# Attention and a mixture of experts on one core: another list of steps, in which no operation changes

## Chip, cores and metric

The kernel runs on one core of a Trainium2 chip. The metric is device time in microseconds from the start to the end of one execution; smaller is better. The engines are TensorE (PE in the rows, with its weight loads as PEld), VectorE (DVE), ScalarE (ACT), GpSimd (POOL) and SyncE (SP), which issues the transfers here.

## What is computed

Causal attention over 8 batches of 8 heads, 576 positions and 64 elements, with a bias from running sums of s; its output, laid out as (8, 576, 512), is the input of a layer of four experts, each a causal attention of its own with 64 elements, of which each position uses the two that a gate ranks highest.

```python
scores = scale * np.matmul(q, k.transpose(0, 1, 3, 2))
cum = np.cumsum(np.maximum(s, 0.0), axis=-1)
bias = -(cum[:, :, :, None] - cum[:, :, None, :])
scores = np.where(causal, -1000000000.0, scores + np.minimum(bias, 0.0))
scores = scores - np.max(scores, axis=-1, keepdims=True)
attn = np.exp(scores)
attn = attn / (np.sum(attn, axis=-1, keepdims=True) + 1e-09)
attn_out = np.matmul(attn, v)
...
logits = x @ w_gate
topk = np.argpartition(-logits, K, axis=-1)[..., :K]
...
for e in range(E):
    q = x @ wq[e]
    k = x @ wk[e]
    v = x @ wv[e]
    ...
    ye = a @ v @ wo[e]
    out += mask[..., None] * w[:, :, kk:kk + 1] * ye
```

## The kernel before

The work is cut into 50 pairs of heads: four pairs for each of the 8 batches of the attention (phase 1), and, one batch later, two pairs of experts for each batch of the second layer (phase 2), whose q, k and v come from projections of the attention's output. Two empty pairs stand between where the last batch has no attention beside it. Slot n of the program, from -2 to 49, holds steps of several pairs, so that the engines always have more than one pair in work: the scores of pair n, the product with v of pair n-1, the maxima of pairs n+1 and n+2, and what comes before and after them.

For one pair the steps and their names in the list are these. Loads: `ld` (L571) brings q and k as "raw", L640 and L641 the q and k of the first pairs as "plain", `lv` (L581, L585) brings v. Splitting: every operand of a score is kept as a rounded high part, q1 and k1, and the rest, q2 and k2. `hi` makes the high parts (`h`, ACT, L679, L689, L720) and copies rows of running sums to k2 (L671); `lo` makes the rest (`l0` to `l3`, DVE, L736 for q and L750 for k in phase 1, L732 and L745 in phase 2) and copies parts with DMAs (L722 and others). Maxima: PE makes scores in bf16 (`m`, L769, and L787 for the diagonal pieces, tiles "mx"), DVE reduces them to a column (`M`, L799, tile "mcol"), PE transposes the nine columns (`mt`, L824), ACT copies them (`mA`, L828, tile "mr") and SP writes them as a row of q2 (`mq`, L841, or L835). Scores: seven banks per pair, each with two passes (`s`, L872 with the high parts and L877 with the rest, whose operands hold the row of maxima; L942 and L946 are the second and third kind of piece). Then ACT makes exponentials (`E`, L916, L918, L925), and POOL sets the upper triangle to zero (`b`, L955) and adds the tiles up into r (`d`, L969 to L977). PE multiplies with v (`v`, L1012, evicted by `V`, L1026) and, for two pairs at once, sums the rows (`a`, L1065, tile "sm", evicted by `A`, L1074). The sums go through DMAs (`r`, L1093, L1102, L1107) and a reciprocal (L1096) to a tile rb, and DVE multiplies with it (L1131). ACT and DVE split the product into a high part and the rest x (L1135 and L1144), and PE projects it (`p`, L1242; tiles "pq", "pw" and "po") to the experts' q and k, to v and the gate, and to the output. Twenty spare steps (`i`, L1486), each of three matmuls of 128x512 on a constant tile, stand in slot -2.

PSUM has eight banks: `take` gives the one that was free for longest, `give` puts one back when its eviction is written down. Which bank a matmul gets, and whose eviction it waits for, therefore follows from the list.

What sets the order of every engine and queue is one list, `ORDER` (lines 82 to 309): 3773 words "slot:step". The program walks through it and calls each step, and every engine and SP run their instructions in the order in which the steps issued them. The loop is:

```python
steps = {n: slot(n) for n in range(-2, N)}
for n, x in order(pairs):
    if x in steps[n]:
        steps[n].pop(x)()
```

Of the kernel before, what the change touches and what calls it, by code (L numbers as in the profile page):

```python
# [47 lines left out]
def pieces(kt, q0, q1):  # L48
# [45 lines left out]
    "2:s2 2:E2 2:b0 -2:i16 2:m4 1:V1 2:s1 2:E1 2:s4 1:m2 2:v0 2:m1 1:w0l 1:d0 2:m3 2:E4 2:d1 2:v3 2:a0 "
    "2:M4 3:lq 2:M3 2:M1 3:lk 1:M2 3:h2 2:a1 2:A1 3:w0l 2:lq 2:m0 3:hc 3:l3 2:A0 2:v1 3:lv 2:mt 2:mA 3:r0 "
    "2:b3 3:m3 3:h3 3:M3 2:v2 3:v0 2:v4 2:b1 2:v5 2:v6 2:v7 2:M0 3:r1 2:mq 2:b2 3:r2 2:d2 3:h1 3:h0 4:m4 "
    "2:m2 2:M2 3:r3 2:V0 3:m2 3:m1 2:V1 3:r4 3:s5 3:E5 3:l1 3:s6 3:E6 3:s0 3:E0 3:s3 3:E3 3:mt 3:mA 3:mq "
    "3:l0 3:l2 2:d0 3:s1 4:l0 4:h0 3:E1 3:s4 3:E4 3:s2 3:E2 3:v1 4:lv 3:v2 3:V0 4:m5 4:h2 3:v3 3:m0 4:M5 "
    "3:M0 2:d3 2:d4 4:lk 3:n0 4:w1f 3:N0 3:v4 4:m3 3:v5 3:M1 4:M4 4:s3 3:b0 4:M3 3:M2 3:n1 4:lq 4:l2 4:v0 "
    "4:E3 4:hc 4:ld 4:h1 3:b2 3:b4 3:b1 4:w0f 3:v6 3:v7 4:s0 4:E0 4:l1 3:o0 3:b3 4:s2 4:E2 4:s4 3:d0 4:mt "  # L100
    "4:E4 4:mA 4:s6 4:E6 3:V1 3:d1 4:h3 4:mq 4:l3 4:w1h 4:w1l 4:s1 3:d2 4:a0 3:d3 3:d4 4:a1 4:A0 4:A1 "
    "4:s5 5:m3 4:v3 4:v4 5:r0 4:E5 5:l2 5:hc 4:E1 4:m2 4:b3 5:r1 5:r2 5:r3 4:v1 4:v2 4:V0 5:lk 5:m5 5:M5 "
    "4:M2 4:v5 4:w0h 4:w0l 4:b1 5:r4 4:m1 5:v3 5:v4 5:m4 3:N1 4:b0 4:d1 5:h3 4:m0 4:v6 5:h0 4:b2 4:b4 "
    "5:s1 5:E1 4:M1 4:M0 5:M4 5:M3 5:h1 4:v7 5:v5 5:v6 5:v7 5:lq 5:s3 4:d2 4:V1 5:h2 4:d3 5:s5 5:E5 5:v0 "
    "5:v1 3:o1 5:v2 5:V0 5:V1 5:s6 5:E6 5:s4 5:E4 5:E3 5:n0 6:w0f 5:s2 4:d4 5:E2 5:s0 5:mt 5:mA 5:n1 5:N0 "
    "5:o0 5:N1 5:E0 5:b0 7:lv 6:lv 5:o1 5:O1 6:m3 6:m5 6:M3 6:M5 5:O0 6:w0h 5:m2 6:lq 5:m1 5:m0 5:M0 3:O1 "
    "5:b2 5:M1 6:m4 6:M4 5:M2 5:l1 5:d1 5:p2 5:P2 5:p0 5:l0 5:mq 5:p3 5:p1 3:O0 5:p6 5:P1 4:d0 6:mt 5:P0 "
    "6:lk 6:l2 6:w1f 5:lv 6:w1h 6:h0 6:l3 6:s6 5:d2 6:E6 6:s1 6:s3 6:E3 6:s2 5:P3 6:E2 6:mA 6:w0l 5:l3 "
    "6:h1 8:ld 5:b3 5:d3 6:mq 5:p4 6:E1 6:b3 6:s5 6:E5 6:b4 6:s0 6:E0 7:ld 6:s4 6:h3 7:lk 5:P6 5:p7 6:l0 "
    "7:l0 7:l1 5:p5 5:P5 5:P4 6:w1l 5:b1 5:d0 6:a0 6:A0 5:b4 5:d4 6:a1 6:A1 7:m3 7:m5 7:M5 5:P7 7:h1 6:l1 "  # L110
    "6:E4 7:r0 6:b2 7:hc 6:v3 6:h2 7:lq 6:v0 6:v1 6:v2 6:b0 6:v4 6:v5 6:v6 6:v7 6:V1 6:V0 6:d1 6:d2 6:m0 "
    "7:r1 7:r2 7:M3 9:ld 7:r3 7:r4 7:s6 7:E6 7:s5 7:E5 7:s0 6:d3 6:M1 6:M2 6:M0 8:h3 7:s3 7:E3 7:b2 6:d4 "
    "7:s1 7:E1 7:s2 7:E2 6:p1 6:P1 6:b1 7:b3 7:E0 7:s4 7:E4 7:b0 7:b1 7:d0 6:hc 7:M4 7:mt 7:mA 7:mq 6:p0 "
    "6:P0 7:h0 8:l1 8:m3 7:l3 7:m0 7:h2 8:m5 7:M0 8:h0 8:p0 7:M1 8:M3 8:M5 8:M4 7:p0 8:P0 8:J0 7:p1 7:d1 "
    "7:v3 7:v4 7:v5 7:l2 8:n0 8:h1 7:b4 8:h2 7:v6 7:v7 7:P1 7:P0 8:L0 8:g0 7:h3 7:M2 8:lq 7:v0 7:v1 7:v2 "
    "8:hc 7:V0 7:V1 7:d2 7:d3 7:d4 8:a1 6:d0 8:a0 8:A0 8:mt 8:mA 8:g2 8:A1 8:s3 8:n1 8:l2 8:lk 8:s0 8:s6 "
    "8:E3 8:E6 8:s5 8:E5 8:s4 8:E4 8:E0 8:l3 8:s1 9:h0 8:b0 8:s2 8:l0 8:N0 8:b1 9:h2 9:r0 9:r1 8:m0 8:mq "
# [12 lines left out]
    "12:m4 12:lq 12:M5 10:M2 11:M3 11:E5 11:m1 11:v6 11:b0 9:O0 11:m0 11:M1 11:v7 10:b1 10:d0 11:v0 13:ld "  # L130
    "11:v1 11:v2 12:m3 11:r1 11:m2 12:M4 11:V0 11:b1 11:d0 11:mt 9:O1 11:mA 12:M3 11:M2 11:b2 12:h2 10:d4 "
# [1458 lines left out]
```

## Time and profile before

| | |
|---|---|
| three runs | 638.54, 637.71, 638.65 us (median 638.54) |
| profiled execution | 637.61 us |
| its span, first to last instruction | 635.6 us |
| granted TensorE clock | 1.000 |
| PE, PEld, DVE, ACT, POOL busy | 99%, 78%, 80%, 74%, 63% |
| chain that ended last, by engine | PE 82%, DVE 7%, ACT 3%, DMA 3%, POOL 2%, SP 2%, issue 2% |

All times of rows come from the profiled execution and count from the first instruction. PE is the engine with the most work; its own rows are therefore read for gaps, and the other engines' rows for what stood behind a gap. The ends of matmuls in the trace are modelled, so an end may lie behind the start of the next one; the starts are the better mark.

### The profile page before, as it was taken

What the parts mean: (1) busy time and instruction counts of PE and PEld (TensorE: products, weight loads), DVE (VectorE), ACT (ScalarE), POOL (GpSimd) and SP (SyncE); (2) the same over time, 40 slices, a digit from 0 to 9 for tenths busy, and PEclk for the clock granted to TensorE, in tenths of its full rate; (3) what the DMA queues carried; (4) which work ended last, traced back from release to release, by engine and by line L of the source; (5) the groups of instructions that cost most, each with busy time, mean ns of one, the idle gap of its engine ahead of it and who ended that gap; (6) DMA issues with size and microseconds to landing.
All of it is one profiled execution on the core that took longest, in us unless ns stands there. A gap on an engine that the chain in (4) does not pass through costs nothing.

```text
span 635.6 us, 15994 instructions
## 1 busy us (share of the span) xinstructions
PE 626.7 (99%) x5517; PEld 498.5 (78%) x5521; DVE 510.9 (80%) x1493; ACT 473.1 (74%) x1159; POOL 401.8 (63%) x511
## 2 busy tenths in 40 slices
PE   8999999999999999999999999999999999999997
PEld 4566798778887888788887888878877878888875
DVE  6888878999978887895788978777878989865884
ACT  3698968857779668778678768887687877676665
POOL 9488568477846766587563886558655875845040
PEclk9999999999999999999999999999999999999999
DMA  8444454345545455574547445553535555333304
GB/s 213 126 136 125 145 153 124 101 119 136 157 127 151 132 133 147 134 188 109 147 119 188 126 124 152 169 145 110 140 89 165 162 134 129 91 98 83 88 1 166
DMA packets 53478, 83.91 MB, mean 132 GB/s; under 512 B 21700, under 2 KB 21700, under 8 KB 53398
## 3 DMA queue, kind: packets, MB, share of 16 engines
q1 hardware_dynamic: 53398, 82.90, 49.2%
q8 instruction: 44, 0.72, 0.5%
q14 instruction: 36, 0.29, 0.1%
HBM read 44.61 MB, written 10.16 MB: 86 GB/s over the span
## 4 chain that ended last, share of the span: by engine, by line
PE 82%; DVE 7%; ACT 3%; DMA 3%; POOL 2%; SPq 2%; issue 2%; DVEq 0%; ACTq 0%; POOLq 0%
PE pvp L1012 17%; PE pq L1242 14%; PE s L872 10%; PE s L877 9%; PE pw L1242 9%; PE po L1242 6%; PE mx L769 5%; PE sm L1065 4%; DVE sink L799 2%; PE mx L787 2%; DVE k L750 1%; PE po L1216 1%; DVE q L736 1%; DVE x L1144 1%; PE mt L824 1%
## 5 line engine op out<-in xcount | busy, mean ns | idle before, releaser
L799 DVE CUSTOM_DVE_ANT_0 sink<-mx,mask 128x64 bf16<-128x64 f32 (+7 forms) x432 | 168.7, 428 | 61.7 <-PE mx L787 28.0
L955 POOL TENSOR_SCALAR_AFFINE_SELECT p<-p 128x256 f32<-128x256 f32 (+1 forms) x192 | 93.8, 500 | 116.4 <-ACT p L916 94.2
L916 ACT ACTIVATE p<-s 128x512 f32<-128x512 f32 (+2 forms) x288 | 140.2, 521 | 24.8 <-PE s L946 11.6
L975 POOL TENSOR_TENSOR r<-r,p 128x640 f32<-128x640 f32 x92 | 125.4, 1364 | 5.3
L872 PE MATMUL s<-q,k 128*128 128x320 f32 (+3 forms) x460 | 125.5, 322 | 0.5 <-issue 0.3
L877 PE MATMUL s<-q,k 97*128 97x320 f32 (+3 forms) x460 | 122.3, 315 | 0.1
L1242 PE MATMUL pq<-x,wqkh 128*128 128x288 f32 x512 | 106.6, 300 | 1.3 <-DVE x L1144 1.1
L1012 PE MATMUL pvp<-p,v 128*64 128x320 f32 (+3 forms) x896 | 94.7, 344 | 0.0
L971 POOL TENSOR_TENSOR r<-p 128x640 f32<-128x640 f32 x46 | 74.6, 1623 | 24.1 <-ACT p L916 23.9
L872 PEld LDWEIGHTS s<-q,k 128*128 128x128 f32 x460 | 79.8, 189 | 10.9 <-issue 2.7
L1242 PEld LDWEIGHTS pq<-x,wqkh 128*128 128x128 f32 x512 | 82.0, 188 | 5.3 <-DVE x L1144 2.0
L877 PEld LDWEIGHTS s<-q,k 97*128 97x128 f32 x460 | 76.7, 190 | 1.3 <-DMA q<-mr 0.7
L1242 PE MATMUL pq<-x,wqkl 128*128 128x288 f32 x256 | 75.6, 295 | 0.0
L1012 PEld LDWEIGHTS pvp<-p,v 128*64 128x64 f32 x896 | 55.8, 137 | 23.5 <-issue 1.5
L955 POOL TENSOR_SCALAR_AFFINE_SELECT r<-p 128x256 f32<-128x256 f32 x48 | 25.8, 538 | 63.0 <-ACT p L918 62.7
L679 ACT ACTIVATE q<-raw 64x576 fp32r<-64x576 f32 x92 | 61.8, 678 | 2.3 <-PE s L905 1.1
L736 DVE TENSOR_TENSOR q<-raw,q 64x576 fp32r<-64x576 f32 x60 | 52.8, 893 | 6.0 <-ACT p L916 3.2
L750 DVE TENSOR_TENSOR k<-raw,k 64x128 fp32r<-64x128 f32 (+1 forms) x60 | 53.1, 900 | 4.0 <-DMA k<-k 2.8
L769 PE MATMUL mx<-k,q 96*64 96x448 bf16 (+7 forms) x600 | 54.6, 294 | 0.2
L1260 ACT ACTIVATE raw<-pq 128x288 f32<-128x288 f32 x64 | 24.9, 407 | 37.2 <-PE pq L1242 37.2
L1242 PE MATMUL pw<-wvgh,x 128*128 128x260 f32 x256 | 51.7, 287 | 0.0
L1026 ACT ACTIVATE pv<-pvp 128x256 f32<-128x256 f32 (+1 forms) x92 | 35.0, 404 | 20.0 <-PE pvp L1012 19.5
(159 smaller groups left out, 1253.1 us busy)
## 6 DMA issues: line engine op xcount, KB each, us to landing
raw<-in_qk_dram SPq DMA_DIRECT2D x30, 576.0 KB
rb<-rr SPq DMA_DIRECT2D x92, 144.0 KB
k<-k SPq DMA_DIRECT2D x40, 288.0 KB
q<-q SPq DMA_DIRECT2D x29, 288.0 KB
v<-in_vm_dram SPq DMA_DIRECT2D x32, 256.0 KB
out_dram<-o SPq DMA_DIRECT2D x32, 256.0 KB
q<-q SPq DMA_DIRECT2D x32, 144.0 KB
k<-k SPq DMA_DIRECT2D x16, 128.0 KB
```

The source lines that it names most:

```text
L679: nc.scalar.activation(q2[0:64, j], x, AF.Copy)
L750: nc.vector.tensor_tensor(part(c[0:64]), get_raw(n)[64:128, :, k], part(c[64:128]).bitcast(F32), op=OP.subtract)
L769: nc.tensor.matmul(t[64 * j : 64 * j + 64, c0 : c0 + k1 - k0], q2[0:RC, 64 * qt : 64 * qt + 64], keys(n, RC, j, k0, k1).bitcast(BF16)[:, 1 ...
L799: nc.vector.tensor_tensor_reduce(sink[:, c0 : c0 + w], t[:, c0 : c0 + w], mask[:, m0 : m0 + w], scale=1.0, scalar=mcol[n][:, 9:10] if bi = ...
L872: nc.tensor.matmul(out, K1[r1(n)][:, span(j, k0, k0 + nk)], Q1[r1(n)][:, j, q0:q1], start=start, stop=stop,)
L877: nc.tensor.matmul(out, K2[r2(n)][0 : RM + 1, span(j, k0, k0 + nk)], Q2[r2(n)][0 : RM + 1, j, q0:q1], start=start, stop=stop,)
L916: nc.scalar.activation(ptile[n][:, j, c : c + w], t[:, 0:w], AF.Exp, scale=0.125)
L955: nc.gpsimd.affine_select(out=a if kt else running()[:, :, 0:128], in_=a, pattern=[[64 if kt == 4 else 0, 2], [1, nk]], compare_op=OP.is_g ...
L971: add(r[:, :, 256:S], p[:, :, 256:576], p[:, :, 896:1216], op=OP.add)
L975: add(r[:, :, q0:S], r[:, :, q0:S], p[:, :, c : c + S - q0], op=OP.add)
L1012: nc.tensor.matmul(cur[h][64 * j : 64 * j + 64, q0 - PVC[h] : q1 - PVC[h]], vsl(j, kt), rtile[n][:, j, 0:128] if own else ptile[n][:, j, c ...
L1242: nc.tensor.matmul(t[0:nk, 0:w], l, r, start=(x == 0), stop=(x == len(terms) - 1))
```

## The change

The list `ORDER` is replaced by another one with the same 3773 steps. The nominal durations from which such a list is sought are accompanied, in the new search, by landings of transfers and durations of instructions that were measured in a trace. No step is added or removed and no instruction changes. Half of the steps move by 11 places or more, the farthest by 224 forward and 300 back.

```diff
--- before.py
+++ after.py
@@ -79,234 +79,234 @@
 ORDER = (
-    "5:w0f -2:i12 -2:i5 -2:i0 -2:i4 -2:i2 -2:f22 -1:z1 -2:i6 -2:c0 -2:i11 -1:z2 -2:z0 -2:h1 -2:c1 -2:c2 "
-    "0:lv -2:i7 -2:f00 -1:ld 0:h1 -2:z2 -2:h0 -2:i8 2:w0f -2:i9 -2:i1 0:h0 -2:f10 -2:i10 -2:c3 -2:hc "
...
+    "-2:id -1:z1 -1:z3 -2:z0 2:w0f -2:i1 -2:i0 -2:i12 -2:i9 -2:i3 -2:i10 -2:i11 -2:i4 -2:lc -2:z1 -2:c0 "
+    "-2:c1 -2:c2 -2:c3 -2:i5 -1:z2 -2:h0 -2:c4 -2:i2 -1:ld -2:i6 -2:i7 -2:i8 -2:h1 -1:z0 -2:f10 0:h2 0:lv "
...
```

Three places, as the engines see them.

The first transfers on SP. `plain` is q and k of the first pair as they stand (L640, L641) with two rows of running sums (L637, from the tile p1); raw2 and raw3 are q and k of later pairs, v0 the first v, s_t the input s, and w_vg1 and w_qk1 are weights. Before:

```order
L488 DMA w_vg1_107<-in_wvg_dram 128x520
L438 DMA s_t_136<-in_s_dram 64x576
L641 DMA plain_130<-in_qk_dram 64x2x576
L581 DMA v0_95<-in_vm_dram 128x512
L585 DMA v0_95<-in_vt_dram 64x64 x2
L571 DMA raw2_157<-in_qk_dram 128x2x576
L640 DMA plain_130<-in_qk_dram 64x2x576
L488 DMA w_qk1_166<-in_wqk_dram 128x512
L637 DMA plain_130<-p1_94 2x1x576 x2
```

and now:

```order
L488 DMA w_qk1_115<-in_wqk_dram 128x512
L438 DMA s_t_163<-in_s_dram 64x576
L640 DMA plain_111<-in_qk_dram 64x2x576
L571 DMA raw2_183<-in_qk_dram 128x2x576
L641 DMA plain_111<-in_qk_dram 64x2x576
L581 DMA v0_95<-in_vm_dram 128x512
L585 DMA v0_95<-in_vt_dram 64x64 x2
L637 DMA plain_111<-p1_94 2x1x576 x2
L640 DMA plain_111<-in_qk_dram 64x2x576
L488 DMA w_vg1_267<-in_wvg_dram 128x520
```

The weights w_vg1 stand behind L637 and w_qk1 in their place ahead of everything; L640 comes third instead of seventh, L641 fifth instead of third.

DVE near the reciprocals of pairs 6 and 7, some 125 to 131 us into the program. x is the rest of the product pv, rb7 the reciprocals, ew, gs and gw belong to the gate, k1 is the high part of k of pair 10, made from raw10. Before:

```order
L1144 TENSOR_TENSOR x_837<-pv4_1070,x_837 128x576
L1144 TENSOR_TENSOR x_837<-pv5_1427,x_837 128x576
L1131 TENSOR_TENSOR pv6_1661<-pv6_1661,rb7_0_1824 128x576
L1334 TENSOR_TENSOR ew0_1645<-ew0_1645,rk0_1686 128x20
L1336 TENSOR_REDUCE gs0_1889<-ew0_1645 128x5
L1337 TENSOR_SCALAR gs0_1889<-gs0_1889 128x5
L1338 RECIPROCAL gs0_1889<-gs0_1889 128x5
L1339 TENSOR_TENSOR gw_99<-ew0_1645,gs0_1889 128x20
L1366 STREAM_TRANSPOSE gwt0_1895<-gw_99 128x32
L750 TENSOR_TENSOR k1_0_66<-raw10_1312,k1_0_66 64x128
L1131 TENSOR_TENSOR pv7_1809<-pv7_1809,rb7_1_1836 128x576
```

and now:

```order
L750 TENSOR_TENSOR k1_0_66<-raw10_1084,k1_0_66 64x128
L1144 TENSOR_TENSOR x_848<-pv5_1422,x_848 128x576
L1131 TENSOR_TENSOR pv6_1660<-pv6_1660,rb7_0_1849 128x576
L1334 TENSOR_TENSOR ew0_1710<-ew0_1710,rk0_1628 128x20
L1336 TENSOR_REDUCE gs0_1866<-ew0_1710 128x5
L1337 TENSOR_SCALAR gs0_1866<-gs0_1866 128x5
L1338 RECIPROCAL gs0_1866<-gs0_1866 128x5
L1339 TENSOR_TENSOR gw_99<-ew0_1710,gs0_1866 128x20
L1366 STREAM_TRANSPOSE gwt0_1871<-gw_99 128x32
L1131 TENSOR_TENSOR pv7_1798<-pv7_1798,rb7_1_1881 128x576
L1144 TENSOR_TENSOR x_848<-pv4_1087,x_848 128x576
```

The short L750 stands ahead of the gate instead of behind it, and the x of pv4 behind both products with rb7. Somewhat later on DVE, where x of pairs 6 and 7, the rest of q and k of pair 10 (L736, L750) and a reduction of the maxima mx11 stand, it was

```order
L1144 TENSOR_TENSOR x_837<-pv6_1661,x_837 128x576
L1144 TENSOR_TENSOR x_837<-pv7_1809,x_837 128x576
L736 TENSOR_TENSOR q1_0_64<-raw10_1312,q2_1_69 64x576
L750 TENSOR_TENSOR k1_0_66<-raw10_1312,k1_0_66 64x1024
L799 ISA sink_80,mcol11_1963<-mx11_1_1981,mask_79 128x384
```

and is now

```order
L1144 TENSOR_TENSOR x_848<-pv6_1660,x_848 128x576
L1144 TENSOR_TENSOR x_848<-pv7_1798,x_848 128x576
L799 ISA sink_80,mcol11_1920<-mx11_1_1946,mask_79 128x384
L799 ISA mcol11_1920 128x1
L799 ISA sink_80,mcol11_1920<-mx11_1_1946,mask_79 128x128
L799 ISA mcol11_1920 128x1
L750 TENSOR_TENSOR k1_0_66<-raw10_1084,k1_0_66 64x1024
L736 TENSOR_TENSOR q1_0_64<-raw10_1084,q2_1_69 64x576
```

The reduction of mx11_1 has moved ahead of L750 and L736.

ACT at the row of maxima of pair 5 (L828, mr5), beside the exponentials of pair 4 (s4) into the tile p0 and the evicted sums rs3. Before:

```order
L918 ACTIVATE p0_93<-s4_0_878 128x2x256
L916 ACTIVATE p0_93<-s4_2_887 128x512
L916 ACTIVATE p0_93<-s4_4_893 128x448
L828 ACTIVATE mr5_900<-mt5_897 9x128
L916 ACTIVATE p0_93<-s4_6_902 128x320
L1026 ACTIVATE pv2_809<-pvp2_1_817 128x320
L689 ACTIVATE k2_0_71<-raw6_572 64x128
L502 ACTIVATE wvgh_84<-w_vg0_835 128x520
L1074 ACTIVATE rs3_932<-sm3_0_920,eps_77 128x288
L1074 ACTIVATE rs3_932<-sm3_1_927,eps_77 128x288
```

and now:

```order
L502 ACTIVATE wvgh_84<-w_vg0_822 128x520
L689 ACTIVATE k2_0_71<-raw6_539 64x128
L1074 ACTIVATE rs3_921<-sm3_0_916,eps_77 128x288
L1074 ACTIVATE rs3_921<-sm3_1_926,eps_77 128x288
L916 ACTIVATE p0_93<-s4_5_893 128x320
L925 ACTIVATE p0_93<-s4_5_893 64x64 x2
L828 ACTIVATE mr5_944<-mt5_914 9x128
L916 ACTIVATE p0_93<-s4_1_899 128x512
L720 ACTIVATE k1_0_66<-raw6_539 64x1024
L720 ACTIVATE k1_0_66<-raw6_539 64x128
```

The copy mr5 has gone from ahead of the two L1074 to behind them and behind the exponentials of s4_5.

## Rows read from the trace of the kernel before

**Rows 1.** The page's first part: busy us (share) and instructions by engine.

```profile
PE 626.7 (99%) x5517; PEld 498.5 (78%) x5521; DVE 510.9 (80%) x1493; ACT 473.1 (74%) x1159; POOL 401.8 (63%) x511
```

**Rows 2.** Stages: stretch us, busy us (count) PE, PEld, DVE, ACT, POOL, clock, DMA, GB/s.

```profile
0.00:16.00 16.00, 13.88 (x69) 6.78 (x70) 10.66 (x29) 5.75 (x8) 14.49 (x34) 1.00 0.87 213
16.00:48.00 32.00, 31.50 (x243) 19.11 (x245) 26.70 (x91) 25.39 (x58) 21.92 (x30) 1.00 0.46 132
48.00:64.00 16.00, 15.24 (x128) 10.04 (x125) 14.26 (x39) 13.70 (x33) 13.29 (x14) 1.00 0.47 130
...
144.00:384.00 240.00, 240.00 (x2204) 196.80 (x2197) 197.25 (x598) 186.61 (x462) 162.92 (x200) 1.00 0.54 141
384.00:600.00 216.00, 215.42 (x1956) 177.03 (x1955) 170.67 (x506) 158.74 (x395) 130.81 (x159) 1.00 0.49 127
```

**Rows 3.** Timeline of PE, start: start, us, instruction, count [idle before, releaser].

```profile
12.04 1.11 PE L769 MATMUL mx<-plain 96*64 96x320 bf16 x14 [0.78 <-DMA plain<-in_qk_dram]
```

**Rows 4.** Timeline of SP's queue at the start.

```profile
8.12 1.42 SPq L637 DMA_DIRECT2D plain<-p  x2
```

**Rows 5.** Timeline of PE from 50 to 64 us.

```profile
50.96 0.33 PE L946 MATMUL s<-q,k 97*128 97x128 f32 x1 [0.26 <-DMA q<-mr]
...
51.94 0.37 PE L872 MATMUL s<-q,k 128*128 128x448 f32 x1
52.15 0.36 PE L877 MATMUL s<-q,k 97*128 97x448 f32 x1
...
57.20 0.47 PE L872 MATMUL s<-q,k 128*128 128x448 f32 x1
57.81 0.47 PE L877 MATMUL s<-q,k 97*128 97x448 f32 x1
...
61.72 1.16 PE L1065 MATMUL sm<-r,ones 128*32 128x288 f32 x12
63.09 0.68 PE L1065 MATMUL sm<-r,ones 128*32 128x288 f32 x4 [0.21 <-POOL r L977]
63.70 0.41 PE L872 MATMUL s<-q,k 128*128 128x320 f32 x1
```

**Rows 6.** Timeline of SP's queue from 44 to 57 us.

```profile
54.99 1.56 SPq L841 DMA_DIRECT2D q<-mr  x2
```

**Rows 7.** Chain of work that ended last: start, us, what, count.

```profile
143.89 1.11 PE sm L1065 x16
...
242.02 2.86 PE pvp L1012 x32
```

**Rows 8.** Timeline of PE from 132 to 141 us.

```profile
134.47 0.41 PE L1242 MATMUL pq<-x,wqkh 128*128 128x288 f32 x1 [1.08 <-DVE x L1144]
...
138.52 0.48 PE L872 MATMUL s<-q,k 128*128 128x320 f32 x2 [0.32 <-issue]
```

**Rows 9.** Timelines of DVE and POOL from 130 to 140 us.

```profile
131.10 3.32 DVE L1144 TENSOR_TENSOR x<-pv,x 128x576 fp32r<-128x576 f32 x2
134.45 2.01 DVE L736 TENSOR_TENSOR q<-raw,q 64x576 fp32r<-64x576 f32 x1
136.49 1.93 DVE L750 TENSOR_TENSOR k<-raw,k 64x1024 fp32r<-64x1024 f32 x1
...
133.88 3.46 POOL L975 TENSOR_TENSOR r<-r,p 128x640 f32<-128x640 f32 x2
```

**Rows 10.** Tile q on DVE: count, ns shortest/median/longest, first and last start.

```profile
L736 DVE TENSOR_TENSOR q<-raw,q x60: 743/754/2012, 17.1 to 534.2; 64x576 fp32r<-64x576 f32 x60
```

**Rows 11.** Chain of work from 46 to 52 us: start, us, what.

```profile
49.15 1.76 DMA q<-mr
```

**Rows 12.** Timeline of PE from 513 to 515 us.

```profile
514.22 0.27 PE L824 MATMUL mt<-ident,mcol 128*9 128x128 f32 x1 [0.23 <-DVE mcol L799]
```

**Rows 13.** Instructions of L1074 on ACT: ns shortest/median/longest.

```profile
L1074 ACT ACTIVATE rs<-sm,eps x46: 478/501/504, 45.8 to 583.3; 128x288 f32<-128x288 f32 x46
```

452 rows, old and new, of the table ORDER are left out of this document.

## The prediction, made before the changed kernel ran

> **What bounds the kernel now.** I read the page's busy shares first, then the table of busy time by stage, then TensorE's (PE's) own rows where something held it up. PE is busy 99% of the span [rows 1]; from 144 to 384 us it shows no idle time at all [rows 2]. So a new order can gain only where PE waits, or where a start that looks busy is not. The page says that PE's ends are modelled: a short wait hides inside "busy". I therefore took waits also from start to start: a matmul that begins later after its predecessor than the same pair of shapes does elsewhere has waited by the difference.
>
> Idle time is recorded at the start, where the first useful matmul comes at 12.04 us [rows 3], then 0.50 us from 16 to 48, 0.76 from 48 to 64 and 0.58 from 384 to 600 [rows 2], and between 1.3 and 1.5 around 134 [rows 8]: one start, two clusters, and single places late. The last 36 us are the chain of the last pair's output; nothing that I could find in the order shortens it, and I put it at zero.
>
> **The change part by part.** All terms are differences. The profiled execution took 637.61 us with a span of 635.6; the median of the three runs is 638.54, 0.93 more. I add the sum to the median. No instruction is added or removed, and the 99% of PE that is work stays as it is.
>
> *Start.* The first maxima matmul waits for a load of q and k, by a recorded 0.78 us [rows 3]. Ahead of the small row copy L637, which the same matmul needs, SP issues two loads of weights; the new order leaves one there (w_qk1, now first) and puts w_vg1 (128x520 in four bytes, 266 KB) behind L637. The load L640 moves from seventh to third place, L641 from third to fifth. In 0 to 16 us the DMA engines are 0.87 busy at 213 GB/s [rows 2], so 266 KB less ahead is worth up to 1.25 us. What is late next is L637: its issue ran from 8.12 for 1.42 us [rows 4], so to 9.54, and a row copy of that kind landed in 1.76 us [rows 11]: 11.3 us against 12.04. The gain lies between 0 (L637 slips too) and 1.0; I take **-0.6**.
>
> *Around 50 to 64 us.* Three waits. At 50.96 a score matmul waits for its row of maxima, 0.26 us; from L872 at 57.20 to the L877 behind it are 0.61 us where the same two shapes stand 0.21 apart at 51.94, so 0.40 of it is a wait that no idle time records [rows 5], since SP issued that row only at 54.99, behind four copies of another chain [rows 6]; from 61.72 sixteen sums last until 63.70, 1.98 us where sixteen take 1.11 [rows 5, 7], so 0.87 for POOL's last addition, of which 0.21 is recorded. Together 1.53. The new order puts more PE work between a row of maxima and its user here and the selects ahead of POOL's additions earlier. I take **-1.3**; the ends are 0 and -1.53.
>
> *Around 130 to 141 us.* Two waits: at 134.47 for x, the difference that DVE makes in L1144, 1.08 us, and at 138.52 for L750, 0.32, which the record calls issue though DVE ended L750 at 138.42 [rows 8, 9]. Sum 1.40. DVE's rows say why they are there: two L1144 took 3.32 us, L736 2.01 and L750 1.93 [rows 9], where L736's median is 0.754 and its longest 2.012 [rows 10]; beside them POOL ran two additions of 3.46 us in all [rows 9]. After the change one DMA less stands ahead of the reciprocal chain on SP (an issue there is 0.78 [rows 6]), the short L750 leaves the stretch between the two reciprocal products and one older L1144 enters it; so the wait for x shrinks by some 0.6. But on PE only two projection groups instead of three now stand before the scores of pair 10, and L750 and L736 go behind one more reduction: that wait grows, by some 0.4 if the DVE instructions there come out shorter. Net **-0.2**, with ends -1.4 (both go) and +1.6 (no less stretched than now: a group of twelve matmuls less, at 2204 in 240 us 1.3, and the reduction, less the 0.6).
>
> The Trainium skill, page "SBUF - State Buffer", section "Who interferes with whom", states that DVE and GpSimd share one pair of ports and that it is an exclusive lock held for the length of an instruction, the loser blocking. The trace agrees in kind: 2.01 us against 0.754 beside POOL's additions. By that rule a measured duration belongs to the pair of instructions that met, not to the instruction, and the term for 130 to 141 us could lie anywhere between its two ends.
>
> *Five single waits behind 384 us.* The last of them is at 514.22, 0.23 us [rows 12]; the stretch records 0.58 in all [rows 2]. In 48 to 64 us the rows above gave 1.53 by starts where 0.47 was recorded beside them, so the five may be worth up to 1.5. Between the last maxima and the transpose that waits for their column the new order has 1.0 to 1.5 us more PE work in two of the five. I take **-1.0**, ends 0 and -1.5.
>
> *What the new order adds.* (a) Pair 5's row of maxima: on ACT its copy (L828) now stands behind two evictions L1074 and the exponentials of one score bank. The sums are done 1.11 us after the transpose [rows 7]; then one L1074 of 0.50 [rows 13], the exponentials some 0.9 (estimate, two of L1074's length less a little), the copy, and 0.8 of issue ahead of a landing of 1.76 [rows 11]: about 5.4 us. PE's work in that time falls from 56 matmuls to 38: sixteen records of sums at 1.11, sixteen two-record products at 2.86 [rows 7], and 14 small ones at up to 0.1: 4.7 to 5.4 us. So a new wait of 0 to 0.7; I take **+0.5**. (b) PSUM banks that are taken again with under 0.9 us of PE work behind the last: 8 before, 13 after. An eviction takes 0.50 [rows 13] and more where ACT has a queue; five new ones at 0 to 0.25 each: **+0.6**. (c) Other moved work of DVE, POOL and SP that meets something new; the median shift is 11 places of 3773, and nothing in the trace shows it: bounded by one more cluster like that at 134 (+1.4), and by none (0), I take **+0.6**.
>
> Sum: -0.6 - 1.3 - 0.2 - 1.0 + 0.5 + 0.6 + 0.6 = -1.4 us. On the median that is **637.1 us**, 0.22% less. About 0.2% (1.3 us) is what a measurement of this kernel can tell from no change.
>
> **The rivals.**
>
> *Nothing gained.* The waits fall and come back in other places. For it: PE is 99% busy, the waits are of a tenth to one us, and each order has had its waits somewhere; (a) to (c) are only what I could see. Against: the clusters at 50 to 64 and 130 to 141 have causes that the order touches. The terms then cancel: 638.5.
>
> *Hidden waits fall.* In 16 to 48 us PE shows 31.50 of 32 us busy, but its weight loads only 19.11 (60%), and in 48 to 64 10.04 of 16 (63%), against 196.80 of 240 (82%) in the steady stretch [rows 2]; also 243 matmuls in 32 us are 0.132 us each, 2204 in 240 are 0.109. If the 19.11 + 10.04 = 29.15 us could go at the steady share, they would take 35.5 us instead of 48. A third of the difference is 4.2 us, which holds the -1.3 of 48 to 64 us already; with the other terms (-0.6 - 0.2 - 1.0 + 1.7 = -0.1) that is -4.3: 634.2. Against it: part of that stretch is other work (maxima of 64 columns, spare matmuls, sums), and the new order leaves the same work there. Half of it, 632.2, is the most that I would expect.
>
> The Trainium skill, page "Perfetto Trace Analysis", section "Identifying the Most-Contended Engine", holds that matmul busy time says little and that the busy share of weight loads is the better measure. This case's trace shows the two apart, 99% and 78%; by the page alone the whole 12.5 us would be open in those 48 us.
>
> *Slower by stretched work.* The new list rests on durations of the old one, and DVE's depend on what POOL does beside it: 0.754 or 2.01 for the same L736. Two more clusters like that of 131 to 138, each 1.4 us on PE's path as there [rows 8, 9], are 2.8, of which (c) holds 0.6; the term there at +1.6 in place of -0.2 is 1.8 more. That makes 4.0 on top of -1.4: +2.6, so 641.1. It decides where DVE's x or k work has under 1.2 us of slack and a POOL addition beside it. Against it: in most of the 48 slots these stretched instructions are there before and hold nobody up (144 to 384 us has no idle PE).
>
> **How the numbers follow.** Forecast 0.42 (0.28 faster, 0.12 the same, 0.02 slower), hidden waits 0.18, nothing gained 0.20 (0.16 same, 0.02 on either side), slower 0.20 (0.18, 0.02 same). Faster 0.48, same 0.30, slower 0.22. The range goes from 632.8 to 641.1: it takes in the hidden-waits case but for its far end, and the slower case up to its centre, which leaves out some 0.15. The likeliest case's own range goes a third of the way to where all terms stand at one end: the good ends are -1.0 - 1.53 - 1.4 - 1.5 = -5.4, so -2.7 and 635.8; the bad ones +1.6 + 0.7 + 1.25 + 1.4 = +5.0, so +0.7 and 639.2.
>
> **What would show it.** The first maxima matmul at 11.3 to 11.6 us; no wait over 0.3 us from 48 to 64; a wait for x at pair 7 of at most 0.6, and one for k of pair 10 of up to 1; a wait for pair 5's row of maxima of some 0.5. If the weight loads' share in 16 to 64 us rises to 70% or more, it is the hidden waits; if new groups of PE idle time stand before DVE's L1144, L736 or L750 with durations near 2 us, it is the slower case. My sum is wrong where waits that no row shows move by more than the 1.7 us of (a) to (c).

## The result: slower, and where the new list lost it

The changed kernel took 644.46 us (median of 11 executions, 639.56 to 647.97), the kernel before 639.12 beside it (11, 637.19 to 642.26). The ratio is 1.0062 with an interval of [1.0034, 1.0091]: 4 us slower (5.3 by the two medians), where 1.4 us faster was forecast. The time lies above the range given.

The profiled execution has a span of 641.8 us. First the page: shares of the span by engine, and the chain that ended last.

```profile
PE 628.6 (98%) x5517; PEld 499.4 (78%) x5521; DVE 522.1 (81%) x1493; ACT 472.7 (74%) x1159; POOL 399.7 (62%) x511
...
PE 81%; DVE 6%; DMA 4%; POOL 2%; ACT 2%; issue 2%; SPq 1%; DVEq 0%; ACTq 0%; POOLq 0%
```

PE's busy time has grown by 1.9 us though its work is the same [rows 1], and DMA now holds 4% of the chain instead of 3%. The table by stage answers [rows 2]; columns as there.

```profile
0.00:16.00 16.00, 14.65 (x68) 6.55 (x69) 11.92 (x32) 7.31 (x11) 14.52 (x34) 1.00 0.72 195
16.00:48.00 32.00, 30.04 (x236) 18.98 (x238) 26.19 (x87) 23.44 (x53) 22.44 (x30) 1.00 0.43 133
48.00:64.00 16.00, 15.11 (x139) 10.98 (x136) 15.45 (x41) 14.02 (x32) 12.24 (x14) 1.00 0.57 166
...
112.00:144.00 32.00, 32.00 (x322) 25.76 (x317) 28.43 (x78) 25.60 (x65) 21.21 (x23) 1.00 0.44 110
144.00:384.00 240.00, 236.72 (x2147) 194.20 (x2147) 203.39 (x592) 182.28 (x452) 160.18 (x196) 0.99 0.54 138
384.00:600.00 216.00, 214.60 (x1934) 173.25 (x1933) 170.12 (x494) 157.37 (x392) 132.92 (x166) 1.00 0.49 128
```

From 112 to 144 us PE has no idle time left: both waits of rows 8 are gone. But from 144 to 384 us, where it had none before, 3.28 us of 240 are idle and the clock is 0.99, from 384 to 600 us 1.40 are idle instead of 0.58, and from 16 to 48 us 1.96 instead of 0.50.

The largest single wait stands at 196 us. Timeline of PE, with one matmul of the same shape as that at 196.03 from later on, and the stage table in steps of 4 us around it:

```profile
193.71 0.44 PE L1012 MATMUL pvp<-r,vx 128*64 128x128 f32 x4
196.03 0.57 PE L872 MATMUL s<-q,k 128*128 128x320 f32 x1 [1.88 <-DVE mcol L799]
196.40 0.31 PE L942 MATMUL s<-q,k 128*128 128x128 f32 x1
196.50 0.58 PE L877 MATMUL s<-q,k 97*128 97x320 f32 x1
...
212.20 0.40 PE L1242 MATMUL pq<-x,wqkh 128*128 128x288 f32 x1 [1.00 <-DVE x L1144]
...
217.70 0.31 PE L872 MATMUL s<-q,k 128*128 128x320 f32 x1
```

```profile
192.00:196.00 4.00, 2.15 (x30) 1.38 (x26) 3.53 (x9) 3.30 (x8) 3.69 (x5) 1.00 0.46 78
196.00:200.00 4.00, 3.97 (x13) 3.42 (x14) 3.53 (x16) 2.02 (x6) 1.90 (x3) 0.57 0.83 241
200.00:204.00 4.00, 4.00 (x36) 3.35 (x36) 3.91 (x7) 2.95 (x8) 0.36 (x1) 1.00 0.19 50
```

PE waits 1.88 us for a bank that DVE's reductions are to free. Right behind it the granted clock is 0.57 in the mean of 4 us: for part of them PE has the lower of its two levels, 1.2 GHz, and a score matmul of 320 columns takes 0.57 us instead of 0.31. That costs (1 - 0.57) x 4 = 1.7 us more in this execution. Whether the wait brought the lower level is not shown; what the runs together say of it stands behind the last experiment.

Why DVE was late at 196 us its own rows tell (timeline of DVE, then of SP's queue, then one row of the chain of work and one of POOL):

```profile
192.43 0.27 DVE L1096 RECIPROCAL sr<-sr 128x18 f32<-128x18 f32 x1 [2.25 <-DMA sr<-rs]
192.61 0.15 DVE L1366 STREAM_TRANSPOSE gwt<-gw 128x32 f32<-128x32 f32 x1
192.78 2.39 DVE L745 TENSOR_TENSOR k<-raw,k 64x512 fp32r<-64x512 f32 x2
195.19 0.62 DVE L799 CUSTOM_DVE_ANT_0 sink<-mx,mask 128x448 bf16<-128x448 f32 x1
```

```profile
183.00 0.59 SPq L571 DMA_DIRECT2D raw<-in_qk_dram  x1
183.64 0.48 SPq L722 DMA_DIRECT2D k<-k  x1
184.16 1.67 SPq L725 DMA_DIRECT2D k<-k  x2
185.94 0.54 SPq L1445 DMA_DIRECT2D out_dram<-o  x1
186.90 0.62 SPq L1093 DMA_DIRECT2D sr<-rs  x1
```

```profile
186.90 5.50 DMA sr<-rs
```

```profile
192.71 1.55 POOL L971 TENSOR_TENSOR r<-p 128x640 f32<-128x640 f32 x1
```

The 9 KB of sums of pair 13 (L1093) are issued behind four bulk transfers (L725 in two DMAs; 1.2 MB in all) and land after 5.50 us. DVE runs its row in order: it stands 2.25 us at the reciprocal L1096, and behind it in the row stand two L745 and then the reductions that PE waits for. The two L745 then meet POOL's L971 and take 2.39 us. The new list has brought these things together: the load L571 for pair 18 went from 147 places ahead of the sums' copy to 18, the reciprocal stands 11 places behind that copy, and the two L745 went from 42 places ahead of the reciprocal to 25 behind it.

The wait for x at 212.20 has the same ingredients (timeline of DVE): DVE waits 1.09 us for the landing of a copy of k, and behind it the difference x takes 2.08 us beside two additions on POOL, where the median of the 32 is 0.759.

```profile
208.76 1.28 DVE L750 TENSOR_TENSOR k<-raw,k 64x128 fp32r<-64x128 f32 x1 [1.09 <-DMA k<-k]
210.07 2.08 DVE L1144 TENSOR_TENSOR x<-pv,x 128x576 fp32r<-128x576 f32 x1
```

They are not the only such places. What DVE waited for in all, after and then before (us in total, times, longest):

```profile
DVE sr L1096 <- DMA sr<-rs: 10.2, 8, 2.8
DVE k L750 <- DMA k<-k: 8.0, 9, 1.4
DVE pv L1131 <- DMA rb<-rr: 7.0, 6, 3.0
```

```profile
DVE pv L1131 <- DMA rb<-rr: 5.5, 7, 1.7
DVE k L750 <- DMA k<-k: 2.8, 3, 1.5
...
DVE sr L1096 <- DMA sr<-rs: 2.0, 3, 0.9
```

Three kinds of landing together held DVE 25.2 us against 10.3. Most of that costs PE nothing by itself. The sum goes with the result throughout: the six lists that came out below a ratio of 1.002, the old one among them, have 10.3 to 14.6 us of it, the seven others 18.5 to 25.2. That is a correlation; no run changes the landings alone.

Executions of one and the same list differ by how long the lower clock was granted: 3 of the 11 of the changed kernel had 1.000 and took 639.6 to 640.6 us, the others 0.992 to 0.997 and 643.5 to 648.0, while of 61 executions of the kernel before, beside eight of the experiments, 21 had 1.000 (636.0 to 639.0) and 34 had 0.997 (median 638.9).

So the two profiles exaggerate: their spans differ by 6.2 us, but the profile of before is one at 1.000 and that of the changed kernel one at 0.997. In the mean over all executions the lower clock takes 2.1 us of the changed kernel and 1.5 us of the kernel before (an estimate: one minus the granted clock, times 640 us).

### The profile page after: what moved, and what is told of

Read it like the earlier page. It is cut to its first block, busy times and chain, and to the rows that moved or that the text cites. A ratio compares the mean times of both kernels' runs of the same rounds, so it can differ in the third digit from the quotient of the medians.

```text
span 641.8 us, 15980 instructions
## 1 busy us (share of the span) xinstructions
PE 628.6 (98%) x5517; PEld 499.4 (78%) x5521; DVE 522.1 (81%) x1493; ACT 472.7 (74%) x1159; POOL 399.7 (62%) x511
## 4 chain that ended last, share of the span: by engine, by line
PE 81%; DVE 6%; DMA 4%; POOL 2%; ACT 2%; issue 2%; SPq 1%; DVEq 0%; ACTq 0%; POOLq 0%
PE pvp L1012 16%; PE pq L1242 14%; PE s L872 10%; PE s L877 10%; PE pw L1242 8%; PE po L1242 7%; PE mx L769 5%; PE sm L1065 4%; DVE sink L799 3%; PE mx L787 2%; DMA k<-k 2%; PE po L1216 1%; PE mt L824 1%; DMA raw<-in_qk_dram 1%; DMA sr<-rs 1%
## 5 line engine op out<-in xcount | busy, mean ns | idle before, releaser
L955 POOL TENSOR_SCALAR_AFFINE_SELECT p<-p 128x256 f32<-128x256 f32 (+1 forms) x192 | 88.8, 474 | 157.6 <-ACT p L916 134.7
L975 POOL TENSOR_TENSOR r<-r,p 128x640 f32<-128x640 f32 (+1 forms) x92 | 125.5, 1365 | 4.9
L1012 PE MATMUL pvp<-p,v 128*64 128x320 f32 (+3 forms) x896 | 93.0, 344 | 0.0
L971 POOL TENSOR_TENSOR r<-p 128x640 f32<-128x640 f32 x46 | 75.2, 1635 | 16.0 <-ACT p L916 15.9
L1012 PEld LDWEIGHTS pvp<-p,v 128*64 128x64 f32 x896 | 57.3, 137 | 26.0 <-issue 0.9
L750 DVE TENSOR_TENSOR k<-raw,k 64x128 fp32r<-64x128 f32 (+1 forms) x60 | 60.4, 1010 | 9.3 <-DMA k<-k 8.0
L736 DVE TENSOR_TENSOR q<-raw,q 64x576 fp32r<-64x576 f32 x60 | 52.4, 885 | 8.8 <-ACT q L679 4.2
L769 PE MATMUL mx<-k,q 96*64 96x320 bf16 (+7 forms) x600 | 54.3, 293 | 0.2
L1026 ACT ACTIVATE pv<-pvp 128x256 f32<-128x256 f32 (+1 forms) x92 | 35.5, 404 | 22.8 <-PE pvp L1012 21.4
L955 POOL TENSOR_SCALAR_AFFINE_SELECT r<-p 128x256 f32<-128x256 f32 x48 | 25.9, 539 | 36.1 <-ACT p L918 35.9
L1242 PEld LDWEIGHTS pq<-x,wqkl 128*128 128x128 f32 x256 | 48.1, 188 | 0.0
```

The lines of the kernel that those rows point to most:

```text
L750: nc.vector.tensor_tensor(part(c[0:64]), get_raw(n)[64:128, :, k], part(c[64:128]).bitcast(F32), op=OP.subtract)
L769: nc.tensor.matmul(t[64 * j : 64 * j + 64, c0 : c0 + k1 - k0], q2[0:RC, 64 * qt : 64 * qt + 64], keys(n, RC, j, k0, k1).bitcast(BF16)[:, 1 ...
L955: nc.gpsimd.affine_select(out=a if kt else running()[:, :, 0:128], in_=a, pattern=[[64 if kt == 4 else 0, 2], [1, nk]], compare_op=OP.is_g ...
L971: add(r[:, :, 256:S], p[:, :, 256:576], p[:, :, 896:1216], op=OP.add)
L975: add(r[:, :, q0:S], r[:, :, q0:S], p[:, :, c : c + S - q0], op=OP.add)
L1012: nc.tensor.matmul(cur[h][64 * j : 64 * j + 64, q0 - PVC[h] : q1 - PVC[h]], vsl(j, kt), rtile[n][:, j, 0:128] if own else ptile[n][:, j, c ...
```

## The experiments

For the mixed lists: the first P steps are taken from one list, then those not yet taken in the order of the other. Two steps that depend on each other stand in the same order in both lists, so they do so in the mixture too. At each seam used only 4 to 7 steps are out of place. Each experiment has its own interval against the kernel before, run beside it. The name in parentheses is the one by which the text refers to it; where there are two, they stand in the order of the two edits.

**The load put behind (ld_late).**

```diff
-... 13:r3 15:ld 14:n0 ... 15:r0 ... 15:r1 ... 15:r2 14:b3 ...
+... 13:r3 14:n0 ... 15:r0 ... 15:r1 ... 15:r2 15:ld 14:b3 ...
```

> The changed list with one step moved: the load of raw q and k for pair 18 (15:ld, 590 KB) goes from 18 places ahead of the first copy of pair 13's sums (15:r0) to behind the last of that chain's DMAs out (15:r2). Theory 1, the queue: the copy of the sums landed 5.50 us after its issue because bulk transfers were ahead of it; now it lands in 2 to 3.5 us, DVE's wait of 2.25 us at L1096 falls under 0.5, the PE wait of 1.9 us near 196 us falls under 0.5, the clock stays at 1.00 from 196 to 200 us, and the median falls by 3 to 4 us to 640 to 641. Theory 2, DVE's row: the copy lands as late as before, nothing changes, 644. Theory 3, the clock falls by itself, whatever waits there are: the PE wait goes, but runs with a clock below 1.00 stay as frequent as in the changed kernel (8 of 11).

Measured: 641.18 us, ratio 1.0032 [0.9997, 1.0066]. DVE's rows at the same place:

```profile
188.59 0.27 DVE L1096 RECIPROCAL sr<-sr 128x18 f32<-128x18 f32 x1
188.77 0.15 DVE L1366 STREAM_TRANSPOSE gwt<-gw 128x32 f32<-128x32 f32 x1
188.94 0.83 DVE L745 TENSOR_TENSOR k<-raw,k 64x512 fp32r<-64x512 f32 x2
```

The sums' copy, issued at 186.05, was there by 188.59; DVE did not wait, its two L745 ran ahead of POOL's next addition in 0.83 us instead of 2.39, and PE was busy for the whole of 184 to 200 us at a clock of 1.00. Without the load among the transfers ahead of it, the landing was not late. A new wait came at 204.74 us, 1.09 us for a select on POOL (L955). The total is 0.3% below that of the changed kernel, less than the two intervals can tell apart.

**The rest of k put ahead (l3_early).**

```diff
-... 15:l2 15:r1 14:v3 ... 14:V1 14:l3 14:M0 ...
+... 15:l2 14:l3 15:r1 14:v3 ... 14:V1 14:M0 ...
```

> The changed list with one step moved: the rest of k of pair 15 (14:l3, two L745 on DVE) goes from behind the reciprocal of pair 13's sums (15:r1) to ahead of it. Theory 1 (only the landing matters): DVE's two L745 run while the sums' copy is under way; it still lands after some 5.5 us, but the reductions behind start some 2 us earlier, so the PE wait near 196 us falls from 1.9 to under 0.5, the clock stays at 1.00 there, 640 to 641. Theory 2 (DVE is short of time there in any order, by stretched L745): the two L745 still take 2.4 us or more, the wait shrinks by less than half, 643 or more. Theory 3 (the clock by itself): runs below 1.00 stay as frequent.

Measured: 640.92 us, 1.0037 [1.0002, 1.0073]. DVE:

```profile
190.57 0.83 DVE L745 TENSOR_TENSOR k<-raw,k 64x512 fp32r<-64x512 f32 x2 [1.12 <-DMA k<-k]
191.43 0.27 DVE L1096 RECIPROCAL sr<-sr 128x18 f32<-128x18 f32 x1
```

Nothing was changed on SP, and the wait at 196 us is gone all the same: theory 1 again, theory 2 falls. One part of theory 1 is not met: the sums' copy, issued at 186.91 behind the same transfers, was there by 191.43, after at most 4.52 us instead of 5.50. Either of the two moves mends the place; in the changed kernel a late landing, an instruction that could have run during it but stood behind it, and a meeting with POOL came together. The total, as above, is not clear of that of the changed kernel.

The third theory, of a clock that falls by itself, is neither shown nor excluded by these two: 5 of 10 and 4 of 10 executions kept 1.000, against 3 of 11. The traces of all the runs together bear it out in part; they stand behind the last experiment.

**The old order from 175 to 215 us (mid_old).**

```diff
-ORDER = new
+ORDER = new up to 1095, old up to 1299, then new
```

> The changed list in which places 1095 to 1299 (some 175 to 215 us) come in the old list's order. Theory 1: this stretch holds 5 of the 6 us by which the changed kernel is slower (two PE waits of 2.1 and 1.2 us and 1.7 us at half the clock): 639 to 640, clock 1.00 in nearly all runs. Rival: the loss is spread over the whole list as many small waits, and the stretch holds a third of it at most: 642 or more.

Measured: 640.48 us, 1.0036 [0.9998, 1.0075]. Between the two expectations: this stretch holds 0.26% of the 0.62%, 1.7 us by the ratios (about 4 us by the plain medians, 644.46 against 640.48), not 5, and the two intervals overlap. So more than half may lie elsewhere. The clock stayed at 1.000 in 4 of 10 executions, not in nearly all.

**New, then old (new_then_old).**

```diff
-ORDER = new
+ORDER = new up to 1095, then old
```

> The changed list up to place 1095 (some 178 us), and from there the remaining steps in the old list's order. By the ledger of PE's starts the new list is 1.6 to 2.0 us ahead there (start and the waits near 134 us gained, 74 us lost): 636.5 to 637.5, below the kernel before. Rival (the gains of the first part are an accident of one profile, or the old rest gives them back): 638.5 to 640.

Measured: 636.10 us, 0.9956 [0.9924, 0.9987], better than both kernels and, with old_new_old below, the fastest of the lists. Up to 178 us the new list gains 2.8 us; all of its loss stands behind.

**The two moves in the old list (old_sr).**

```diff
-... 15:ld ... 14:l3 ... 14:b3 15:r0 15:r1 14:p1 ...
+... 14:b3 15:ld 15:r0 15:r1 14:l3 14:p1 ...
```

> The list of before with two steps moved, as the changed list has them: the load of raw q and k for pair 18 (15:ld) just ahead of the first copy of pair 13's sums (15:r0), and the rest of k of pair 15 (14:l3) behind the reciprocal (15:r1). Theory 1 (these two make the wait near 196 us): the copy lands 4 us or more after its issue, DVE stands idle for 1 to 2.5 us at L1096 with L745 and reductions behind it, and PE waits 0.5 to 2 us between 190 and 202 us; where it waits over 1 us the granted clock falls behind that and costs some 1.7 us more: 639.5 to 642. Rival (the old list has slack enough behind it: the reductions of pair 16 stand 20 places further back): DVE waits, PE doesn't, 638.5.

Measured: 637.65 us, 0.9971 [0.9943, 0.9999]. The rival was right. DVE did wait:

```profile
192.68 0.27 DVE L1096 RECIPROCAL sr<-sr 128x18 f32<-128x18 f32 x1 [1.07 <-DMA sr<-rs]
192.98 0.83 DVE L745 TENSOR_TENSOR k<-raw,k 64x512 fp32r<-64x512 f32 x2
```

but PE did not (it is busy for the whole of 186 to 202 us). The copy, issued at 190.50 right behind the load, landed after some 2.1 us, not 5.5, so the load alone does not make it late: in the new list three more bulk transfers stood between. And the reductions stood further back. The two moves are harmless in this list.

**Old, then new, from 215 us (old_then_new).**

```diff
-ORDER = old
+ORDER = old up to 1299, then new
```

> The list of before up to place 1299 (some 215 us), from there the remaining steps in the new list's order. Theory 1: the second part of the new list is slower by itself, by some 3 us in small waits behind DVE (mt35 near 434, the product and projection near 502 to 511): 641 to 642, with a clock like that of before. Rival: the second part is as good as the old one, and all of the 6 us come from 175 to 215 us and the clock behind: 638 to 639.

Measured: 641.35 us, 1.0049 [1.0015, 1.0082]. The second part of the new list is 3 us slower by itself.

**Old, then new, from 385 us (tail_new).**

```diff
-ORDER = old
+ORDER = old up to 2360, then new
```

> The list of before up to place 2360 (some 385 us), from there the new order. The kernel old_then_new, new from 215 us on, was 2.9 us slower than before. If that sits mostly behind 434 us (mt35, the product and projection near 502 to 511): 640 to 641. If it is spread evenly over 215 to 600 us: 639.5. If it sits ahead of 384 us (k and q of pairs 18, 23 and 26): 638.5.

Measured: 641.97 us, 1.0046 [1.0013, 1.0079]. Almost all of those 3 us stand behind 385 us. Two of its waits (timeline of PE), then the sums of busy time from 384 to 600 us, of this list and of before:

```profile
437.33 0.28 PE L824 MATMUL mt<-ident,mcol 128*9 128x128 f32 x1 [0.57 <-DVE mcol L799]
...
507.02 0.53 PE L1242 MATMUL pq<-x,wqkh 128*128 128x288 f32 x2 [0.35 <-ACT pv L1026]
```

```profile
sum 216.00, PE 214.52 PEld 173.15 DVE 168.95 ACT 157.34 POOL 129.81; mean PE 53.63 PEld 43.29 DVE 42.24 ACT 39.34 POOL 32.45
```

```profile
sum 216.00, PE 215.42 PEld 177.03 DVE 170.67 ACT 158.74 POOL 130.81; mean PE 53.85 PEld 44.26 DVE 42.67 ACT 39.69 POOL 32.70
```

From 384 to 600 us PE has lost only 0.9 us of busy time, but 3.9 us of weight loads. The measured loss, 3 us, is nearer to the second number; the two windows do not hold quite the same work, as this profile stands some 2.5 us later at 384 us. The Trainium skill, page "Perfetto Trace Analysis", section "Identifying the Most-Contended Engine", prefers the weight loads' share to the matmuls'; here the trace agrees with it. Compared by the amount of PE's work done (an estimate from the starts of all matmuls), this list falls back by some 1.2 us between 420 and 440 us and by some 1.4 between 480 and 510, around the two waits shown, and the changed kernel does the same. In the profile of old_then_new the first of the two waits is missing, and the list is as slow; so it is not that wait alone.

**Two gains of the first part, taken singly (old_new_old, best_mix).**

```diff
-ORDER = old
+ORDER = old up to 439, new up to 1095, then old
```

> The list of before up to place 439 (some 72 us), the new order up to place 1095 (some 178 us), then the old one. Theory 1: the new list's gain before 178 us lies in the waits near 134 us that it takes away (2 us), and the waits of the old list up to 72 us are no longer than the new one's: 635 to 636. Rival: the start and 48 to 64 us bring the gain, and this kernel has only what is left, 637.5 to 638.5.

Measured: 637.00 us, 0.9953 [0.9926, 0.9980]; no idle time is recorded on PE from 132 to 142 us. The median lies between the two expectations; by the ratio, 3.0 us below before, theory 1 holds. The new list's gain in the first part comes from behind 72 us, where the waits for x and k stood, and the start and 48 to 64 us add nothing that can be told apart.

```diff
-ORDER = old
+ORDER = new up to 64, old up to 439, new up to 1095, then old
```

> As the list old_new_old, but with the new list's first 64 places (to some 16 us), in which the first maxima start 0.4 to 0.9 us earlier, and the old order behind them up to place 439, in which the row of maxima of pair 0 is issued 11 places earlier than in the new one. If the two gains add up: 0.4 to 0.9 us under the kernel old_new_old, 634 to 635.5. If the seam costs a wait or the earlier start runs into the next landing: no less than old_new_old.

Measured: 637.86 us, 0.9993 [0.9950, 1.0036]. The earlier start did not add to the gain; in its profile three waits stand from 19 to 23 us in its place, the last for the row of maxima of pair 0.

**Waits mended by hand (first_mended, new_mended).**

```diff
 new up to 1095, then old, and
-... 1:w0l ... 1:M2 2:mt ...   4:w0l ... 5:M3 5:mt ...   3:N0 3:V0 ...
+... 1:M2 1:w0l 2:mt ...       ... 5:M3 4:w0l 5:mt ...   3:V0 3:N0 ...
```

> The list new_then_old (new up to place 1095, then old) with three steps moved by a few places: the rest of the weights wqkl (1:w0l and 4:w0l, DVE, L507, two instructions of 1.0 us each) from ahead of the reductions to behind them, before the transposes mt3 and mt6; and the eviction of the product of pair 3 (3:V0, ACT, L1026) from behind the copy of x (3:N0, 0.9 us) to ahead of it. Theory: the PE waits of 1.0 us at mt3, 0.85 us at the fourth score bank of pair 4 and 1.1 us at mt6 that every profile of the new list's first part shows are set by these three rows, and fall to 0.3 or less each: 2 to 2.5 us less, 633.5 to 634.5, and 633 with the clock at 1.00 throughout. Rival: what they hid comes next (another reduction, another bank), under 1 us gained, 635 to 636.

Measured: 640.00 us, 1.0012 [0.9981, 1.0043]: 3.6 us slower, by the two ratios, than without the moves. The waits at mt6 and at the bank of pair 4 are gone as expected, that at mt3 (0.81 recorded) is not. Two others came: 0.98 at mt4, and 1.41 at 81 us for x, with the clock falling right behind it (timeline of PE, and the stage table):

```profile
81.19 0.40 PE L1242 MATMUL pq<-x,wqkh 128*128 128x288 f32 x1 [1.41 <-DVE x L1144]
...
82.50 0.44 PE L1242 MATMUL pq<-x,wqkl 128*128 128x288 f32 x1
```

```profile
80.00:84.00 4.00, 2.57 (x11) 2.34 (x12) 3.68 (x12) 2.57 (x5) 1.98 (x3) 0.75 0.84 239
84.00:88.00 4.00, 4.00 (x27) 4.00 (x27) 3.87 (x16) 1.76 (x5) 2.94 (x3) 0.83 0.69 220
```

The clock costs (0.25 + 0.17) x 4 = 1.7 us in this execution as well. The rival was right, and more than right: what came in place of the waits was longer than they were.

```diff
 new, with those three moves, and
-... 15:r1 ... 14:l3 ...   34:l3 ... 33:M1 ...   40:h3 39:V0 ... 39:N0 ... 39:v7 39:V1 ...
+... 14:l3 15:r1 ...       ... 33:M1 34:l3 ...   39:V0 40:h3 ... 39:v7 39:V1 ... 39:N0 ...
```

> The whole new list with the three moves of the kernel first_mended, the one of l3_early (14:l3 ahead of 15:r1), and three of the same kind further back: the rest of k (34:l3, DVE, L750) behind the reductions ahead of mt35, and the two evictions of the product of pair 39 (39:V0, 39:V1, ACT, L1026) ahead of a copy of k and of the copy of x. Theory 1 (a handful of rows carries the loss): seven waits of 0.3 to 2.1 us go, some 6.5 us, and the new list comes out at 636 to 637.5, below before. Rival (many small waits, the list is tight everywhere): 639 or more.

Measured: 641.98 us, 1.0043 [1.0011, 1.0076]. The wait at mt35 (0.57 recorded in the changed kernel) and the one of 1.88 us are gone, but the list as a whole stays slower than before, as the rival said. It doesn't prove the rival: three of the seven moves are those of first_mended, which had cost 3.6 us there; the other four were never run without them. Between 640 and 642 is where every other version of the list with the new tail ended.

What the traces say of the clock, then. In three pairs of profiles the list is the same up to the stretch in question, and one of the two falls to the lower level there while the other doesn't. Stage tables of before and of tail_new, then that of new_mended, whose partner is the row from 80 to 84 us of first_mended above:

```profile
24.00:28.00 4.00, 4.00 (x36) 2.32 (x34) 3.16 (x13) 2.19 (x5) 3.78 (x5) 1.00 0.44 161
```

```profile
24.00:28.00 4.00, 4.00 (x15) 2.28 (x15) 1.53 (x6) 1.24 (x4) 2.56 (x4) 0.57 0.56 207
```

```profile
80.00:84.00 4.00, 2.50 (x19) 1.86 (x14) 2.71 (x4) 2.25 (x6) 0.62 (x2) 1.00 0.82 196
```

Before and tail_new have a longest recorded wait of 0.20 us each from 17 to 28 us; only tail_new falls. first_mended falls behind 1.41 us, new_mended does not behind 1.25. The changed kernel and new_then_old wait 0.87 and 0.88 us near 22 us; only the second falls. In all, seven of the thirteen profiles have such a stretch, and four of these (tail_new and new_mended near 25 us, old_new_old and old_then_new between 615 and 625) have no recorded wait over 0.2 us in the 6 us ahead of it. So the clock does fall without a long wait; that a long wait ever brought it down is not shown.

The parts do not add up: the first part -0.44%, 175 to 215 us +0.26%, behind 385 us +0.46% make +0.28%, and +0.62% was measured. Each part has an interval of about 0.35% to either side. At a granted clock of 1.000 they come closer: the medians there (3 to 5 executions of each kernel, 32 of before) are 637.3 us before, 635.3 for new_then_old, 639.0 for mid_old, 640.7 for old_then_new, 641.6 for tail_new and 640.6 for the changed kernel. That is -2.0 for the first part, +1.5 for 175 to 215 us and +3.4 from 215 us on, together +2.9, where the changed kernel has +3.3. So the loss is there without the lower clock, and by these few executions most of it lies in the late part of the list.

## Why the prediction was wrong, point by point

- **What bounds the kernel**: right. PE's work is the same, and the difference is waits on it and the time at its lower clock. The clock was not in the sum at all; it is a small part of the difference (2.1 us against 1.5 in the mean), though 1.7 of the 6.2 us between the two profiles.
- **Start**, -0.6: 0.4 came. The first maxima matmul now stands at 11.64 us instead of 12.04, with no wait, just behind the span expected (11.3 to 11.6). What was late next was missed: at 21.56 us PE waits 0.87 for the row of maxima of pair 0, more than the start had gained, and the gain was not seen in any total.
- **50 to 64 us**, -1.3: two of the three waits went; the sums still last from 61.82 to 63.80, 1.98 us as before [rows 5]. A wait of 0.69 us for a bank behind ACT's L1026 at 59.40 is new. The 0.66 that went came back in it, and recorded idle time from 48 to 64 us rose from 0.76 to 0.89: next to nothing of the term came.
- **130 to 141 us**, -0.2: the sign was right, the size at the good end. PE is busy for all of 32 us; the wait for k that I expected to grow is not there.
- **Single waits behind 384 us**, -1.0: here the prediction failed most. The sign is wrong: 1.40 us of recorded idle time instead of 0.58, and the new tail in the old list costs 2.9 us [0.8 to 5.0]. That is an error of 4 us, of some 5.4 in all. This term looked only at the waits that the old trace had, and the list was replaced everywhere; no term was put for new waits there but a share of (b) and (c).
- **(a) pair 5's row**, +0.5: no wait came. **(b) banks**, +0.6: waits behind ACT's L1026 came (0.69 at 59.40 and 0.35 near 508 the longest, 1.04 together).
- **(c) other moved work**, +0.6, bounded by 1.4: the second step that failed. In the profile the wait at 196 us alone is 1.88 and the wait for x behind it 1.00; by the totals the stretch from 175 to 215 us costs about 1.7 us. The bound was taken from the worst cluster of the old trace, as if a new list could not make a worse one. It could have been read: each reciprocal L1096 waits for a landing with DVE's row behind it, and how many places stand between L1093 and L1096, and which reductions stand behind, is in the order.
- **The rivals**: "slower by stretched work" gave 641.1 us and a chance of 0.20. Its sign was seen at 212 us, where PE waits 1.00 for an L1144 of 2.08 us. At 196 us stretched instructions took part too: two L745 in 2.39 us beside POOL's addition, 0.83 without it. The rule of the Trainium skill, page "SBUF - State Buffer", section "Who interferes with whom", agrees with that. But its mechanism was half of it; the late landings were missing. "Hidden waits fall" is excluded: weight loads from 16 to 64 us are 29.96 us of 48, before 29.15.

The first part of the list taken alone tests the method: for the places before 178 us the terms were -0.6 - 1.3 - 0.2 + 0.5 = -1.6 us, and -2.8 us were measured there. That the sum is near is luck: the gain lies behind 72 us, where the trace shows the 1.40 us of rows 8 gone, the one place where I gave almost none. The prediction also took 0.2% as what a measurement can tell; the intervals came out at about 0.3% to either side.

What stays open: which rows make the 3 us behind 385 us (two waits of 0.57 and 0.35 us are named, the other recorded ones are under 0.3 each, and no run mends these alone), how much of the loss is late landings, and what brings the lower clock.

## What to carry to other kernels

When a list is replaced as a whole, do not price it by the waits that the old trace shows: walk each in-order engine past every instruction that waits for a landing, and ask what stands behind it and who needs that. Measured landings and durations belong to the neighbours they were measured with: the same copy behind the same transfers took 5.50 us in one trace and at most 4.52 in another. Mixed lists (one up to a place, then the other) cost little to make and tell which part wins; here the first part of the new list and the rest of the old one, 0.9956 [0.9924, 0.9987], beat both, while mending single waits by hand did not. Before a loss in one profile is put down to the clock, see whether the other profile happens to be one without such a stretch.

## What the runs showed of the hardware

- In seven of the thirteen profiles the granted clock has one stretch at the lower level, 1.2 GHz, while PE has work, and each time it costs 1.7 us (one minus the granted clock, summed over the stretch). Shortly ahead of it PE had waited 1.88 us (the changed kernel), 1.41 (first_mended), 0.88 (new_then_old), and in four profiles no more than 0.2. With the same list it came in one execution and not in another.
- A copy of 9 KB took 5.50 us to land behind four bulk transfers that were issued in the 3.9 us before it, at most 4.52 us behind the same transfers in another kernel (l3_early), and at most 2.6 us with one of them taken out of its way (ld_late); with the same load right ahead of it in the old list it took some 2.1 us (old_sr).
- Two subtractions of 64x512 on DVE took 0.83 us without POOL's addition beside them and 2.39 us with it.
